# Loading q once, splitting streamed weights on chip, and larger k, v and w_out transfers in a linear-attention and feed-forward kernel

## The chip, the core and the metric

The kernel runs on one core of a Trainium2 chip. A core has TensorE (PE, matrix products), VectorE (DVE), ScalarE (ACT), GpSimd (POOL) and SyncE (SP); each works through its own instructions in order and waits for others by semaphores. Transfers between HBM and on-chip memory are issued by SyncE and GpSimd here and run on 16 shared transfer engines. The metric is device microseconds of one execution, the median of three runs.

## The reference

What is computed, cut to what matters (8 batches, 8 heads, 576 positions, head size 64; w_in is 512 x 2048 and w_out 2048 x 512, both float64 and read as pairs of 32-bit words):

```python
kv = np.einsum('bhsd,bhse->bhde', k, v)
out = np.einsum('bhsd,bhde->bhse', q, kv)
rms = np.sqrt(np.mean(out * out, axis=-1, keepdims=True) + 1e-06)
x = (out / rms * g_norm).transpose(0, 2, 1, 3).reshape(4608, 512)
h = x @ w_in
g = h * np.tanh(np.log1p(np.exp(h)))      # mish
return g @ w_out
```

## The kernel before

**Two parts.** The first part makes x from q, k and v, multiplies it by w_in, applies mish and stores g to HBM (gd, gp). The second part reads g back and multiplies it by w_out. The tokens lie in 9 tiles of 512; tile 0 is done whole, tiles 1 and 2 singly, and tiles 3 to 8 in three pairs. The second part works on 18 groups of 256 tokens.

**Seven products.** Both matmuls use a scheme with seven block products instead of eight (A11, S1, S2, S4, A12, S3, A22 of the left side against T1, T3, T2, T4, B11, B21, B22 of the right side). T1, T2, T3 and T4 are differences of the weight's four blocks. Each factor is kept as a high and a low half: `split` casts the high half on ScalarE and subtracts it on VectorE (L210 to L212), and a product has three terms of them.

**Places.** The first part is a row of 256 places, one block product in each. Place 0 is the first product of w_in; tile 0 takes places 0 to 31, tiles 1 and 2 take 28 each, and each pair 56 (from 88, 144 and 200). All other work (a load, a transpose, a cast) is a named step, and the table `WHEN` gives each step its place; what stands at negative places comes ahead of the first product. The table alone sets the order of the instructions on every engine; nothing is reordered later. Names: `k3.mul0` is the product of k and v of batch 3 for the first four heads, `x4.1.transpose` a step of tile 4 for the second four heads, `w5.load` a block of w_in, `o3.load` a chunk of w_out, `s1.4` a streamed w_in.

**The weights.** w_in has 8 blocks of columns. Four forms of each (B11, B21, T4, B22) stay on chip in `wfb`. The three others (T1, T3 and T2) stay for six blocks in pages `wfa` and `wfc`; blocks 6 and 7 share theirs with the stream. Each block's split forms, 12 x 128 columns, are stored to HBM (`wid`) by GpSimd (L283, L284). For each pair of tiles six blocks are streamed back: `stream` (L288) issues two transfers straight into the pages of blocks 6 and 7, high and low halves as they are, once TensorE is done with the page. w_out is read in 16 chunks of 128 x 512 (L231), scaled by ScalarE (L222), joined from word pairs by VectorE (L217 to L219), differenced (L225 to L227), and stored to HBM (`wod`) by three GpSimd transfers each (L316 to L318).

**Attention.** k and v come in pieces of 128 x 576 (L327), with three buffers each. q of a tile comes from tile 2 on as `qs`: VectorE's transpose (L446) works on 32 x 32 squares, so each 32 partitions hold one half of the head's 64 columns, and q is loaded twice, shifted by 32 columns (L429, eight transfers where a tile spans two batches). The 1/rms row `fl` (ScalarE, ln and exp, L509 and L510) is stored to `rd` (L514), read back spread over the partitions (L520), and multiplied into x by VectorE (L528).

**Queues.** SyncE issues the loads, the stores of 1/rms and the loads of what they spread; GpSimd issues the stores of g (L723, L728, L731; L669 for tile 0), of `wid` and of `wod`. The tiles for mish, `ula`, `ulb` and `ur`, have two buffers each. `put_in` (L725) adds into them on VectorE, ScalarE applies mish (L208).

Of the kernel before, what the change touches and what calls it, by code (L numbers as in the profile page):

```python
# [8 lines left out]
F32 = mybir.dt.float32  # L9
F32R = mybir.dt.float32r  # L10
U32 = mybir.dt.uint32
# [6 lines left out]
T1, T3, T2, T4, B11, B21, B22 = range(7)  # L18
# [6 lines left out]
    "w1.load": -57.761, "w1.scale": -57.665, "kv.a": -56.646, "rows.a": -56.517, "w0.load": -55.073, "kv.mul.a": -54.701,  # L25
    "rows.b": -50.685, "constants": -49.286, "kv.b": -48.206, "kv.keep.a": -46.532, "x0.0.transpose": -44.158,
# [95 lines left out]
def linear_attention_rms_mish_ffn(  # L122
# [169 lines left out]
    def weight_out(c, h):  # L292
# [14 lines left out]
        def join():  # L307
            join_words(st["x"], st["w"])
# [999 lines left out]
```

## Time and profile before

| What | Value |
|---|---|
| Runs | 819.5, 820.7 and 824.51 us, median 820.7 |
| Profiled execution | 819.2 us, its span 817.4 us |
| Busy share of the span | TensorE 96%, VectorE 71%, ScalarE 54%, GpSimd 13% |
| Granted TensorE clock, mean | 0.988 |
| Moved | 181.09 MB |

The profiled execution is one execution on the chip, its span from the first to the last instruction. Matmuls are pipelined, so a busy TensorE is not TensorE at its peak. A line number is that of the kernel before. "Idle before" is the time in which an engine had nothing to do just ahead of an instruction, and the name behind the arrow is what ended it. The granted clock is a share of full speed, 2.4 GHz; 0.5 of it is 1.2 GHz.

### The profile page before, as it was taken

The numbers are of one execution on the slowest core, as the hardware profiler recorded it, in microseconds if no ns is written. First come the engines' busy times: TensorE is split into PE (matmuls) and PEld (weight loads), VectorE is DVE, ScalarE is ACT, GpSimd is POOL, SyncE is SP. The second block draws the span as 40 slices with busy tenths as digits, with TensorE's granted clock in tenths as the row PEclk, the third lists the DMA queues.
The fourth block names the chain that finished last, engine by engine and source line by source line (L and its number), as shares of the span: only waits on it lengthen the run. The fifth ranks groups of instructions, "written<-read, shape, count | busy, mean of one in ns | idle before, by whom it ended". The sixth has DMA issues, their size and how long they took to land.

```text
span 817.4 us, 14052 instructions
## 1 busy us (share of the span) xinstructions
PE 781.9 (96%) x5456; PEld 660.7 (81%) x5456; DVE 578.5 (71%) x714; ACT 441.6 (54%) x641; POOL 104.0 (13%) x191
## 2 busy tenths in 40 slices
PE   3999999989998999899999999999999999999997
PEld 2677898879766777678888998888888888888886
DVE  2887846468436785658436788888888888877885
ACT  3877765746635475466547664444444444445442
POOL 1021321122213222332111100000000000000000
PEclk9999999989999999999999999999999999999999
DMA  9998979999998968989679653344444444444401
GB/s 269 278 326 268 360 273 317 286 272 304 321 317 275 318 223 285 291 314 321 231 255 340 209 194 129 129 141 128 146 130 152 134 126 154 134 140 152 142 27 52
DMA packets 118434, 181.09 MB, mean 222 GB/s; under 512 B 18720, under 2 KB 80160, under 8 KB 118368
## 3 DMA queue, kind: packets, MB, share of 16 engines
q1 hardware_dynamic: 102848, 128.74, 51.4%
q0 software_dynamic: 15424, 51.39, 16.8%
q8 instruction: 43, 0.70, 0.4%
q14 instruction: 23, 0.19, 0.1%
q10 hardware_dynamic: 96, 0.07, 0.0%
HBM read 119.21 MB, written 60.95 MB: 220 GB/s over the span
## 4 chain that ended last, share of the span: by engine, by line
PE 80%; DMA 9%; issue 5%; ACT 2%; SPq 1%; DVE 1%; POOL 1%; ACTq 0%; POOLq 0%; DVEq 0%
PE a L1061 15%; PE bc L1061 11%; PE a L690 10%; PE a L1066 8%; PE bc L690 7%; PE bc L1066 6%; PE a L680 5%; PE bc L680 3%; PE a L658 3%; PE q L1209 2%; PE bc L658 2%; PE x L468 2%; DMA wod<-wx 2%; DMA qs<-in_q_dram 2%; DMA wfa<-wid 2%
## 5 line engine op out<-in xcount | busy, mean ns | idle before, releaser
L725 DVE TENSOR_TENSOR ula<-bc,ula 128x512 f32<-128x512 f32 x32 | 22.0, 687 | 43.5 <-PE bc L690 24.8
L208 ACT ACTIVATE ur<-ur 128x1024 f32<-128x1024 f32 x32 | 33.9, 1059 | 31.2 <-DVE ur L725 31.1
L690 PE MATMUL bc<-wfa,wfa 128*128 128x512 f32 x144 | 37.4, 395 | 6.3 <-DVE ula L725 3.6
L690 PE MATMUL a<-wfc,wfc 128*128 128x512 f32 x96 | 34.9, 405 | 3.7 <-ACT ula L607 3.4
L690 PEld LDWEIGHTS bc<-wfa,wfa 128*128 128x128 f32 x144 | 26.8, 188 | 13.8 <-DVE ula L725 4.1
L690 PE MATMUL a<-wfa,wfb 128*128 128x512 f32 x144 | 37.1, 393 | 0.0
L690 PE MATMUL bc<-wfc,wfb 128*128 128x512 f32 x144 | 36.9, 392 | 0.0
L620 ACT COPY ur<-a 128x512 f32<-128x512 f32 x32 | 18.8, 586 | 32.8 <-PE a L690 28.3
L211 ACT CAST wfa<-g 128x1024 fp32r<-128x1024 f32 (+1 forms) x24 | 23.8, 998 | 21.5 <-PE a L1066 7.8
L211 ACT CAST wfc<-wfb 128x1024 fp32r<-128x1024 f32 x23 | 24.0, 1051 | 20.9 <-PE a L1066 11.7
L212 DVE TENSOR_TENSOR wfa<-g,wfa 128x1024 fp32r<-128x1024 f32 (+1 forms) x24 | 27.5, 1154 | 9.4 <-ACT wfa L211 9.4
L208 ACT ACTIVATE ula<-ula 128x512 f32<-128x512 f32 x32 | 20.2, 633 | 25.3 <-DVE ula L725 25.0
L690 PE MATMUL a<-pc,wfb 128*128 128x512 f32 x96 | 33.9, 393 | 0.0
L690 PE MATMUL a<-pb,wfa 128*128 128x512 f32 x96 | 33.7, 391 | 0.0
L690 PE MATMUL bc<-pa,wfb 128*128 128x512 f32 x96 | 33.6, 390 | 0.0
L690 PEld LDWEIGHTS a<-wfa,wfb 128*128 128x128 f32 x144 | 26.7, 188 | 8.2 <-issue 2.5
L690 PEld LDWEIGHTS bc<-wfc,wfb 128*128 128x128 f32 x144 | 27.1, 189 | 6.8 <-issue 1.1
L211 ACT CAST wfa<-wfb 128x1024 fp32r<-128x1024 f32 x19 | 19.9, 1052 | 21.5 <-PE a L1066 15.5
L725 DVE TENSOR_TENSOR ur<-a,ur 128x512 f32<-128x512 f32 x32 | 21.9, 685 | 11.8 <-PE a L690 8.1
L1116 DVE TENSOR_TENSOR ur<-ow 128x1024 f32<-128x1024 f32 x16 | 19.6, 1225 | 14.1 <-ACT ow L1113 14.1
L212 DVE TENSOR_TENSOR wfa<-wfb,wfa 128x1024 fp32r<-128x1024 f32 x19 | 23.1, 1220 | 8.9 <-ACT wfa L211 8.9
L211 ACT CAST wfc<-g 128x1024 fp32r<-128x1024 f32 x17 | 17.7, 1051 | 17.2 <-PE a L1066 11.7
(524 smaller groups left out, 2454.7 us busy)
## 6 DMA issues: line engine op xcount, KB each, us to landing
gp<-ur POOLq DMA_DIRECT2D x24, 512.0 KB, 6.2
g<-gp SPq DMA_DIRECT2D x12, 1024.0 KB
wfb<-gp SPq DMA_DIRECT2D x12, 1024.0 KB
wfa<-wid SPq DMA_DIRECT2D x18, 512.0 KB
w<-in_moe_w_out_dram SPq DMA_DIRECT2D x32, 256.0 KB
km<-in_k_dram SPq DMA_DIRECT2D x28, 288.0 KB
vm<-in_v_dram SPq DMA_DIRECT2D x28, 288.0 KB
gp<-ula POOLq DMA_DIRECT2D x24, 256.0 KB, 4.7
```

What stands on the lines that cost most here:

```text
L208: nc.scalar.activation(o, i, AF.Mish)
L211: nc.scalar.copy(hi, src)
L212: nc.vector.tensor_sub(lo, src, hi.bitcast(F32))
L468: nc.tensor.matmul(st["x"][a][half(o), c], kv[r], st["q"][r, a, c], start=True, stop=True)
L620: then(t + 4, lambda: nc.scalar.copy(dst(st, "12"), st["a"]))
L658: nc.tensor.matmul(banks[m], w[:, a, kc, :], xf[b][:, kc], start=r == kc == s == 0, stop=(r == kc == 1 and s == 2), skip_group_check=True,)
L680: nc.tensor.matmul(bank[:, jj * TH:(jj + 1) * TH], w[:, a, kc, :], xf[b][:, kc], start=first and jj == kc == s == 0, stop=(kc == 1 and s = ...
L690: nc.tensor.matmul(bank, w[:, a, kc, :], xf[b][:, kc], start=first and kc == s == 0, stop=(kc == 1 and s == 2), skip_group_check=True,)
L725: nc.vector.tensor_add(o, bank_view(st, block, bank), o)
L1061: nc.tensor.matmul(bank.rearrange("p (s h n) -> p s h n", s=2, h=2), gf[0][:, c], wo_form(c, right), start=first and c == 0, stop=False, s ...
L1066: nc.tensor.matmul(halves(bank)[:, 0], gf[1][:, c], wo_form(c, right)[:, 0], start=False, stop=c == NF2 - 1, skip_group_check=True)
L1116: nc.vector.tensor_add(st["o"].rearrange("p r (c n) -> p (r c) n", c=2), a[:, :, 0], a[:, :, 1])
```

## The change

**q.** Each 32 partitions' first half loads the whole run of 64 columns; a new step `double` (GpSimd, two copies of 32 x 32 x 32) writes the second half from it. Transfers per load fall from eight to four, or from four to two where a tile lies in one batch.

**Streamed w_in.** `wid` keeps the three differences whole (6 x 128 columns, stored from `wd`), and `split_ring` makes both halves on chip, into one ring page `tr` of blocks 6 and 7. For the first two pairs a step `load` brings them into a page `ws` of its own; for the third into the lower half of the ring page itself.

**k, v and w_out.** k and v are 128 x 2 x 576 in one transfer, two buffers for k and one for v. w_out comes in 8 chunks of twice the size, each scaled and joined in two steps, with one buffer, and is stored by two transfers; the forms lie as 7 x 256 columns, so a form's order on the right side changes (B21 ahead of B11).

**1/rms.** It is stored four times over and read as rows of both heads' 1024 values.

**Places.** Every entry of `WHEN` is new, among them the step that loads ScalarE's table for ln and exp. The core of the diff:

```diff
-    "table.exp": -43.37, "x0.0.turned": -42.175, "w1.join": -41.998, "w2.load": -38.422, "w4.load": -38.247,
+    "table.exp": 139.787, "s1.1.load": 140.314, "f5.1.0": 140.744, "x7.0.project": 140.822, "f5.4.0": 141.698,
...
-    kvp = part1.enter_context(tc.tile_pool(name="kvp", bufs=3))
+    kvp = {name: part1.enter_context(tc.tile_pool(name=name + "p", bufs=n)) for name, n in (("k", 2), ("v", 1))}
...
+    def split_ring(n, src):
+        t = ring(n).rearrange("p (s n) -> p s n", s=2)
+        split(t[:, 0], t[:, 1], src)
...
         def store():
-            c = j % 2 * FORM
-            nc.gpsimd.dma_start(wid[j][:, 0:PAGE], page(f"wfa{j}").bitcast(F32))
-            nc.gpsimd.dma_start(wid[j][:, PAGE:], page(f"wfc{j // 2}")[:, c:c + FORM].bitcast(F32))
+            nc.gpsimd.dma_start(wid[j], st["d"][:, 0:3].rearrange("p f n -> p (f n)"))
...
-    def stream(j, n):
-        nc.sync.dma_start(page(f"wfa{NF2 - 2 + n}").bitcast(F32), wid[j][:, 0:PAGE])
-        nc.sync.dma_start(page(f"wfc{NQ - 1}")[:, n * FORM:(n + 1) * FORM].bitcast(F32), wid[j][:, PAGE:])
+    def stream(j, n, staged):
+        st = {}
         def load():
+            st["t"] = pools["ws"].tile([P, 6 * P], F32, name="ws") if staged else ring(n)[:, 6 * P:].bitcast(F32)
+            nc.sync.dma_start(st["t"], wid[j])
+
+        return load, lambda: split_ring(n, st["t"])
...
+    def kv_load(name, b, n):
+        t = kvp[name].tile([P, 2, 9 * D], F32, name=name + "m")
+        src = (k if name == "k" else v)[b, 4 * n:4 * n + 1]
+        nc.sync.dma_start(t, bass.AP(src.tensor, src.offset, [[9 * D, P], [2 * S * D, 2], [1, 9 * D]]))
+        return t
...
-            for i in (0, 2, 1, 3):
+            for i in (0, 2):
...
-                    src = q[b, 4 * u + i // 2, s0:s0 + 1, R * (i % 2):]
-                    src = bass.AP(src.tensor, src.offset, [[run, R], [(3 - 2 * (i // 2)) * S * D, 2], [1, run - R]])
+                    src = q[b, 4 * u + i // 2, s0:s0 + 1]
+                    src = bass.AP(src.tensor, src.offset, [[run, R], [(3 - i) * S * D, 2], [1, run]])
...
+        def double():
+            t = qs[u].rearrange("p a (c d) -> p (a c) d", d=D)
+            for i in (0, 2):
+                nc.gpsimd.tensor_copy(t[(i + 1) * R:(i + 2) * R, :, 0:R], t[i * R:(i + 1) * R, :, R:])
...
-    step("pools.wx", start(3), pools_of(("w64", 2), ("wx", 1)))
+    step("pools.wx", start(3), pools_of(("w64", 1), ("wx", 1), ("ws", 1)))
```

New places that the prediction speaks of: the products k2.mul1 34.88, k3.mul0 39.55 and k3.mul1 44.25; k5.mul1 81.43, k6.mul0 85.13 and k6.mul1 90.17. The splits s0.6 at 135.93, s1.4 at 178.72, s1.5 at 185.47 and s2.2 at 220.70, whose forms are first used at places 138, 180, 187 and 222. The loads of q and their copies x6.0 at 91.09 and 91.65, x7.0 at 114.03 and 114.98, x8.1 at 159.65 and 161.66.

**How it moves instructions.** First SyncE's queue around the 1/rms of tiles 3 and 4 (rd is the row's store, fh and fa its spread; rd_111 is tile 3's row before, rd_114 after). Before:

```order
L429 DMA qs<-in_q_dram 32x2x608
L429 DMA qs<-in_q_dram 32x2x352
L514 DMA rd_112<-fl 2x512 x4
L520 DMA fh<-rd_111 64x2x512 x2
L520 DMA fa<-rd_112 64x2x512 x2
L231 DMA w_2128<-in_moe_w_out_dram 128x2x256 x2
```

After:

```order
L558 DMA rd_114<-fl 8x1x512 x4
L565 DMA fh<-rd_114 64x1x1024 x2
L467 DMA qs<-in_q_dram 32x2x640
L467 DMA qs<-in_q_dram 32x2x384
L467 DMA qs<-in_q_dram 32x2x640
L467 DMA qs<-in_q_dram 32x2x384
L325 DMA w_2005<-in_moe_w_out_dram 128x1024 x2
L565 DMA fa<-rd_114 64x1x1024 x2
```

The spread of tile 3's first half stood behind a q load of eight and another tile's stores; it now stands behind its own stores, and a q load of four behind it.

Second, ScalarE ahead of the first product (fa and fh hold squares and then 1/rms of tile 0's two halves; the first product needs pa, and wfb_308 before, wfb_332 after). Before:

```order
L474 ACTIVATE fa<-x_229 128x1024
L211 CAST wfb_247<-wfa_133 128x4x256
L504 ACTIVATE fa<-a,eps 128x512 x2
L505 ACTIVATE fa<-fa 128x1024
L211 CAST wfb_308<-wfa_227 128x4x256
L369 COPY kv_120<-s_119 128x128
L452 COPY wfa_142<-ss 128x512
L452 COPY wfa_142<-bc 128x512
L211 CAST pa_327<-x_305 128x1024
```

After:

```order
L547 ACT_TABLE_LOAD
L547 ACTIVATE fa<-a,eps 128x512 x2
L548 ACT_TABLE_LOAD
L548 ACTIVATE fa<-fa 128x1024
L407 COPY kv_123<-s_122 128x128
L214 CAST wfb_296<-wfa_216 128x4x256
L495 COPY wfa_151<-ss 128x512
L495 COPY wfa_151<-bc 128x512
L225 ACTIVATE wfa_304<-w_228 128x1024
L214 CAST pa_318<-x_293 128x1024
L520 ACTIVATE fh<-bc 128x512 x2
L225 ACTIVATE wfa_328<-wfb_231 128x1024
```

Two table loads have come in, and the scaling of the weight for the first product, which stood ahead of the squares, now stands behind both copies of q.

Third, GpSimd's queue at the end of tile 2 and in the first pair. Before:

```order
L731 DMA gp_89<-ur 128x1024
L723 DMA gp_89<-ulb 128x512
L316 DMA wod_101<-wx 128x128
L317 DMA wod_101<-wx 128x2x128
L318 DMA wod_101<-w_2479 128x512
L728 DMA gp_89<-ula 128x512
```

After:

```order
L776 DMA gd_91<-ur 128x1024
L472 COPY qs<-qs 32x32x32 x2
L768 DMA gd_91<-ulb 128x2x256
L773 DMA gp_92<-ula 128x512
L776 DMA gp_92<-ur 128x1024
L355 DMA wod_104<-w_2485 128x1024
L356 DMA wod_104<-wx 128x768
L768 DMA gp_92<-ulb 128x512
```

Where three stores of converted w_out stood between two stores of g, there are two now, and at other places a pair of copies of q.

## Rows read from the trace of the kernel before

**Rows 1.** The page, part 1: busy us, share of the span, instructions
```profile
PE 781.9 (96%) x5456; PEld 660.7 (81%) x5456; DVE 578.5 (71%) x714; ACT 441.6 (54%) x641; POOL 104.0 (13%) x191
```

**Rows 2.** Table by stage: length, busy us by engine, PEclk, transfers' share, GB/s
```profile
0.00:31.50 31.50, 17.23 (x187) 11.63 (x188) 13.24 (x15) 16.37 (x21) 2.62 (x15) 1.00 0.97 294
31.50:345.00 313.50, 296.58 (x2689) 242.12 (x2688) 206.76 (x293) 188.47 (x294) 73.55 (x126) 0.97 0.92 293
345.00:460.00 115.00, 114.85 (x512) 93.95 (x511) 68.47 (x104) 71.10 (x113) 26.71 (x48) 1.00 0.80 278
460.00:817.40 357.40, 353.27 (x2073) 312.95 (x2071) 290.06 (x305) 165.71 (x215) 1.08 (x2) 1.00 0.43 134
```

**Rows 3.** TensorE's waits: waited for, us in total, times, longest
```profile
PE s L351 <- DMA wfb<-in_v_dram: 11.1, 1, 11.1
PE bc L680 <- ACT ur L612: 3.9, 1, 3.9
PE bc L690 <- DVE ula L725: 3.6, 1, 3.6
PE a L690 <- ACT ula L607: 3.4, 1, 3.4
PE bc L690 <- DMA wfa<-wid: 2.7, 2, 1.9
PE ss L362 <- DMA vm<-in_v_dram: 2.5, 1, 2.5
```

**Rows 4.** The same table, just behind four of these waits
```profile
124.60:130.00 5.40, 5.40 (x99) 4.43 (x100) 2.58 (x3) 0.08 (x1) 0.00 (x0) 0.68 1.06 279
178.00:186.00 8.00, 7.95 (x45) 7.95 (x46) 7.58 (x10) 3.38 (x7) 2.25 (x4) 0.63 0.97 290
247.60:254.00 6.40, 6.36 (x99) 4.59 (x100) 5.45 (x8) 3.32 (x5) 2.69 (x5) 0.73 1.06 308
334.60:340.00 5.40, 5.33 (x18) 4.32 (x19) 2.48 (x5) 2.65 (x6) 2.88 (x5) 0.73 0.83 240
```

**Rows 5.** SyncE's queue, then the chain of waits, 157 to 178: start, us, what
```profile
159.87 6.52 SPq L429 DMA_DIRECT2D qs<-in_q_dram  x8
...
170.82 4.29 DMA fh<-rd
```

**Rows 6.** The chain of waits, 205 to 250
```profile
235.90 5.55 issue
241.46 5.43 DMA gp<-ulb
```

**Rows 7.** The chain of waits, 100 to 180
```profile
118.69 5.75 DMA vm<-in_v_dram
```

**Rows 8.** The page, part 6: transfers, how many, KB each
```profile
wfa<-wid SPq DMA_DIRECT2D x18, 512.0 KB
```

**Rows 9.** Groups of ScalarE and VectorE (busy us, mean ns); ScalarE in order of time
```profile
L211 ACT CAST wfb<-wfb 128x768 fp32r<-128x768 f32 x1 | 0.8, 845 | 0.0
L212 DVE TENSOR_TENSOR wfb<-wfb 128x768 fp32r<-128x768 f32 x1 | 1.0, 951 | 0.0
L217 DVE TENSOR_SCALAR wfa<-wfa 128x1024 uint32<-128x1024 uint32 x8 | 5.5, 691 | 17.7 <-ACT wfa L222 17.7
...
161.16 1.28 ACT L508 ACT_TABLE_LOAD   x1
162.60 0.69 ACT L509 ACTIVATE fl<-ss,eps 128x512 f32<-128x512 f32 x1 [0.15 <-issue]
```

**Rows 10.** Groups of GpSimd: busy us, mean ns, idle before
```profile
masks.py:199 POOL TENSOR_SCALAR_AFFINE_SELECT ident<-ident 128x128 f32<-128x128 f32 x1 | 0.3, 287 | 0.1
L791 POOL MEMSET ones<- 128x128 f32 x1 | 0.2, 194 | 0.0
```

**Rows 11.** ScalarE and TensorE in order of time, first 40 us
```profile
23.92 1.06 ACT L505 ACTIVATE fa<-fa 128x1024 f32<-128x1024 f32 x1
...
30.48 3.33 PE L658 MATMUL a<-pa,wfb 128*128 128x512 f32 x12
```

More of the change, by code (lines that the diff above doesn't have):

```diff
@@ L17 @@
 A11, S1, S2, S4, A12, S3, A22 = range(7)
-T1, T3, T2, T4, B11, B21, B22 = range(7)
+T1, T3, T2, T4, B21, B11, B22 = range(7)
 PROD = ((A11, B11, "a"), (S1, T1, "c"), (A22, T4, "p"), (S2, T2, "a"), (A12, B21, "b"), (S4, B22, "c"), (S3, T3, "a"))
@@ L24 @@
 WHEN = {
-    "w1.load": -57.761, "w1.scale": -57.665, "kv.a": -56.646, "rows.a": -56.517, "w0.load": -55.073, "kv.mul.a": -54.701,
-    "rows.b": -50.685, "constants": -49.286, "kv.b": -48.206, "kv.keep.a": -46.532, "x0.0.transpose": -44.158,
[90 rows of a table removed]
+    "kv.a": -58.068, "constants": -56.889, "rows.a": -56.704, "w1.load": -56.033, "kv.mul.a": -55.141, "kv.b": -54.793,
[93 rows of a table added]
 }
@@ L235, in forms, with ring, in_ring @@
         return t.rearrange("p (f s m n) -> p f s m n", s=2, m=2, n=P)
+    rings = {}
+    def ring(n, dtype=F32R, fresh=False):
+        if fresh or n not in rings:
+            rings[n] = wfp.tile([P, 3 * FORM], dtype, name=f"tr{n}")
+        return rings[n]
+    def in_ring(t):
+        return t.rearrange("p (s f m n) -> p s f m n", s=2, f=3, n=P)
+    def split_ring(n, src):
+        t = ring(n).rearrange("p (s n) -> p s n", s=2)
+        split(t[:, 0], t[:, 1], src)
     def w_form(j, f, streamed=None):
@@ L239, in w_form @@
             return forms(wb[j])[:, RESIDENT.index(f)]
-        j = j if streamed is None else NF2 - 2 + streamed
+        n = j - (NF2 - 2) if streamed is None else streamed
+        if n >= 0:
+            return in_ring(ring(n))[:, :, f]
         return forms(page(f"wfc{j // 2}"))[:, j % 2] if f == T2 else forms(page(f"wfa{j}"))[:, int(f == T3)]
@@ L255, in scale @@
         def scale():
-            st["x"] = page(f"wfa{j}", F32, True)
+            st["x"] = ring(j - (NF2 - 2), F32, True)[:, 0:PAGE] if j >= NF2 - 2 else page(f"wfa{j}", F32, True)
             scale_words(st["x"], st["w"])
@@ L275, in sums @@
         def sums():
-            page(f"wfa{j}", F32R, True)
-            parts(forms(page(f"wfa{j}")), st["d"][:, 0:2])
-            parts(forms(page(f"wfc{j // 2}"))[:, j % 2:j % 2 + 1], st["d"][:, 2:3])
+            if j >= NF2 - 2:
+                ring(j - (NF2 - 2), F32R, True)
+                split_ring(j - (NF2 - 2), st["d"][:, 0:3].rearrange("p f n -> p (f n)"))
+            else:
+                page(f"wfa{j}", F32R, True)
+                parts(forms(page(f"wfa{j}")), st["d"][:, 0:2])
+                parts(forms(page(f"wfc{j // 2}"))[:, j % 2:j % 2 + 1], st["d"][:, 2:3])
@@ L292, in weight_out, with load @@
-    def weight_out(c, h):
+    def stream(j, n, staged):
         st = {}
-        whole = wod[c][:, h]
         def load():
-            srcs = []
+            st["t"] = pools["ws"].tile([P, 6 * P], F32, name="ws") if staged else ring(n)[:, 6 * P:].bitcast(F32)
+            nc.sync.dma_start(st["t"], wid[j])
+        return load, lambda: split_ring(n, st["t"])
+    def weight_out(c):
+        st = {}
+        def load():
+            st["w"] = pools["w64"].tile([P, 2, 8 * P], U32, name="w64")
@@ L315, in store @@
-        def store():
-            nc.gpsimd.dma_start(whole[:, B11:B11 + 1], st["x"][:, 0:1])
-            nc.gpsimd.dma_start(whole[:, B21:B22 + 1], st["x"][:, 1:4:2])
-            nc.gpsimd.dma_start(whole[:, T1:T4 + 1], st["d"])
-        return load, scale, join, differences, store
-    def kv_load(b, hp):
-        ts = []
-        for name, src in (("km", k), ("vm", v)):
-            t = kvp.tile([P, 9 * D], F32, name=name)
-            src = src[b, 2 * hp:2 * hp + 1]
-            nc.sync.dma_start(t, bass.AP(src.tensor, src.offset, [[9 * D, P], [1, 9 * D]]))
-            ts.append(t)
-        return ts
+                nc.sync.dma_start(st["w"][:, 1 - fh], w_out[f0:f0 + P, :])
@@ new lines, in words, with blocks, scale, join @@
+        def words(r):
+            return st["w"].rearrange("p f (r n t) -> p r f n t", r=2, t=2)[:, r]
+        def blocks(r):
+            return st["x"][:, r]
+        def scale(r):
+            if "x" not in st:
+                st["x"] = pools["wx"].tile([P, 2, 2, G], F32, name="wx")
+            nc.scalar.mul(blocks(r), words(r)[:, :, :, 1].bitcast(F32), 2.0 ** -112)
+        def join(r):
+            w, t = words(r), blocks(r).bitcast(U32)
+            low, high = w[:, :, :, 0], w[:, :, :, 1]
+            nc.vector.tensor_single_scalar(t, t, 3, ALU.logical_shift_left)
+            nc.vector.scalar_tensor_tensor(t, high, 0x80000000, t, ALU.bitwise_and, ALU.bitwise_or)
+            nc.vector.scalar_tensor_tensor(t, low, 29, t, ALU.logical_shift_right, ALU.bitwise_or)
@@ L331, in half @@
+        return {
+            "load": load, "scale0": lambda: scale(0), "scale1": lambda: scale(1), "join0": lambda: join(0),
+            "join1": lambda: join(1), "diff": differences, "store": store,
+        }
+    def kv_load(name, b, n):
[3 more added lines that the diff above has]
+        return t
     def half(o, turned=False):
@@ L528, in normalize @@
                 nc.vector.tensor_mul(o, o, st["rr"])
-        return {f.__name__: f for f in (load, transpose, turned, project, square, scaled, sums, rstd, keep, spread, normalize)}
+        return {f.__name__: f for f in (load, double, transpose, turned, project, square, scaled, sums, rstd, keep, spread, normalize)}
     def x_block(j, r, h):
@@ L853, in linear_attention_rms_mish_ffn @@
             step(f"k{b}.keep{n}", t + made[n] + 1, lambda b=b, n=n: k_keep(b, n))
-        for p in range(4):
-            step(f"k{b}.load{p}", t + loads[p], lambda b=b, p=p: k_load(b, p))
+            for m, name in enumerate("kv"):
+                step(f"k{b}.{name}{n}", t + loads[n] + 0.001 * m, lambda name=name, b=b, n=n: k_load(name, b, n))
     def attention(j, t, steps):
@@ L862, in attention @@
             else:
+                if j >= T32 and "transpose" in names:
+                    step(f"x{j}.{u}.double", t + n - 0.01, lambda u=u: do(j, u, "double"))
                 for m, name in enumerate(names):
@@ L923, in linear_attention_rms_mish_ffn @@
     step("pools.xt", t1 + 18, pools_of(("xt", 1)))
-    step("pools.wx", start(3), pools_of(("w64", 2), ("wx", 1)))
-    places = [start(3) + n for n in (13, 20, 26)] + [start(j) + n for j in (4, 5, 6) for n in (3, 8, 13, 20, 26)][:13]
-    for i, t in enumerate(places):
-        def chunk(i=i, s=0):
-            if s == 0:
-                conv["out", i] = weight_out(i // 2, i % 2)
-            conv["out", i][s]()
-        for s, n in zip(range(5), (-5, 0, 0.01, 1, 2)):
-            step(f"o{i}.{('load', 'scale', 'join', 'diff', 'store')[s]}", t + n, lambda i=i, s=s, chunk=chunk: chunk(i, s))
+    step("pools.wx", start(3), pools_of(("w64", 1), ("wx", 1), ("ws", 1)))
+    for c in range(NF2):
+        t = start(3) - 11 + 15 * c
+        conv["out", c] = weight_out(c)
+        for n, name in zip((0, 5, 5.1, 6, 6.1, 7, 8), ("load", "scale0", "join0", "scale1", "join1", "diff", "store")):
+            step(f"o{c}.{name}", t + n, lambda c=c, name=name: conv["out", c][name]())
     gs = [{"s": s, "f": {}, "mm": None} for s in range(NG)]
@@ L965, in place2 @@
                 wb[int(name[3:])] if name.startswith("wfb")
-                else up.tile([P, FORM], F32R, name="ula") if name == "ula" else page(name)
+                else up.tile([P, FORM], F32R, name="ula") if name == "ula" else ring(int(name[2:])) if name.startswith("tr") else page(name)
             )
@@ L1156, in linear_attention_rms_mish_ffn @@
         for n in range(1, NF2 - 1):
-            step(f"s{i}.{n}", start(SINGLE + 2 * i) + 7 * n, lambda j=order[n + 1], n=n: stream(j, (n + 1) % 2))
+            t = start(SINGLE + 2 * i) + 7 * n
+            for (name, m), f in zip((("load", -6 if i < 2 else -0.5), ("split", -0.4 if i < 2 else 1)), stream(order[n + 1], (n + 1) % 2, i < 2)):
+                step(f"s{i}.{n}.{name}", t + m, f)
     for t in sorted(t for t in plan if t < 0):
```

74 lines of the change are left out of this document (37 added, 37 removed), and 183 rows, old and new, of tables (WHEN, homes).

## The prediction

> **What bounds the kernel now.** I read the busy shares first, then a table by stage, then the list of what TensorE waited for, then the chain of waits around its longest stops. TensorE is busy 781.9 us of a span of 817.4 [rows 1]. By stage [rows 2]: in the first 31.5 us TensorE works 17.2; from there to 345 it loses 16.9 us, with the transfer engines at 0.92 of their time; from 345 to 460, where they have fallen to 0.80, it loses 0.15. Behind 460 us (the second matmul, which keeps its instructions) it loses 4.1, with the transfer engines at 0.43. So the kernel is bound by TensorE, and what a change of transfers and places can give is the start and the stops up to 345 us.
>
> TensorE's own list names the stops [rows 3]: 11.1 us for the first k and v, and in the middle 3.9, 3.6, 3.4, 2.7 (twice a wait, 1.9 the longest) and 2.5: **16.1 us**. After four of them the granted clock is low [rows 4]: 0.68, 0.63, 0.73 and 0.73 over 5.4, 8.0, 6.4 and 5.4 us, that is stretches at 1.2 instead of 2.4 GHz behind a stop, worth 1.7 + 3.0 + 1.7 + 1.5 = **7.9 us**. Together the middle holds 24.0 us that a perfectly fed kernel would not spend. The start is a separate sum.
>
> Why it stops. The 3.9 us at 174 to 178: the queue of SyncE issues eight pieces of a q load for 6.52 us, and only behind them the piece of 1/rms that a normalize waits for, which needs 4.29 us more; VectorE is held in its order by that normalize [rows 5]. The 3.6 us at 244 to 248: GpSimd's queue stands 5.55 us at a store of converted w_out, the store of a mish tile behind it lands 5.43 us after its issue, and VectorE needs that tile's room [rows 6]. The chain of the 3.4 us at 331 to 335 reads the same way, through the room of a chunk of w_out. The 2.7 us are two streamed w_in pages that came late, the 2.5 us a v load that came 5.75 us after its issue [rows 7].
>
> **The change part by part.** The sum is made against the profiled execution: 819.2 us, of which the span is 817.4. The median of the three runs, 820.7, is 1.5 above that, and I add it at the end.
>
> *Fewer bytes.* A streamed w_in is 12 x 128 columns of 4 bytes, 786 KB, moved eighteen times, the first 512 KB of it by the transfers of [rows 8]; whole instead of in two parts it is half: 7.1 MB less read, and 3.1 MB less stored for the eight w_in blocks. q is read once instead of nearly twice: some 6 MB less, and four issues per load instead of eight in full segments. That is 16 MB of the some 133 that the rates of [rows 2] give for the first 460 us, an eighth, and would bring 0.92 near the 0.80 at which TensorE no longer waited. w_out comes in 8 chunks instead of 16, with two stores each instead of three, so GpSimd's queue has 16 places of the kind of [rows 6] instead of 48. In the new order the first half of 1/rms of tile 3 stands directly behind its store, ahead of the q load that was in front of it. Each of the five causes is thus weakened or gone: I book **-24.0**, and what comes back as new terms (bounds: 0, if the waits are of order and not of bytes, and -24.0).
>
> *Splitting on chip.* Eighteen splits, each a cast of 845 ns on ScalarE and a subtraction of 951 ns on VectorE [rows 9]: 15.2 and 17.1 us of work. Between 31.5 and 460 us ScalarE works 259.6 of 428.5 us and VectorE 275.2 [rows 2], so they fit beside TensorE. The cover is gone where a split is recorded little ahead of its product. Two thirds of them (the first two pairs of tiles) load into a page of their own some products early, which takes the late pages of [rows 3] away; but the splits s0.6, s1.4, s1.5 and s2.2 stand 1.3 to 2.1 places ahead of their first use. 256 places lie between 30.48 us [rows 11] and 460, 1.68 us each, so they have 2.2 to 3.5 us for 1.8 us of work that stands behind other work on both engines. I take one of them late by all of it, **+2** (bounds 0 and four times 1.8, 7.2).
>
> *v with one buffer.* k and v come as 128 x 2 x 576 in one transfer; k has two buffers, v one. So v of a pair of heads can't be asked for until the product before it has read its v. At four of them (k3.mul0, k3.mul1, k6.mul0, k6.mul1) the next product stands 3.7 to 5 places behind, 6.2 to 8.4 us, and the nearest row has 5.75 us from issue to landing for half these bytes [rows 7]. I take one stop of the size of the old one with its clock, 2.5 + 1.7: **+4.2** (bounds 0 and four, 16.8).
>
> *GpSimd copies.* 28 copies of 32 x 1024 elements, two ahead of each VectorE transpose. The trace has no such copy. Nearest are 287 ns and 194 ns for 128 columns [rows 10]: eight times the larger is 2.3 us, and if all of the smaller were fixed cost a copy is 0.2. Between them 1.2, so 34 us on an engine that is busy 104 of 817. What counts is order: a copy waits for its q, and a mish store behind it waits too. I take two thirds of one stop like that of [rows 6], 3.6 + 1.7: **+3.5** (bounds 0 and three such stops, 15.9).
>
> *The start.* k and v now go ahead of w_in's 1.05 MB, which at the 294 GB/s of [rows 2] is 3.6 us earlier than 11.1. But the step that loaded one table for both ln and exp has moved from place -43 to 139.8, and each 1/rms of tile 0 now loads a table twice, 1.28 us each [rows 9]: exp, which ended at 24.98 [rows 11], ends at 24.98 - 3.6 + 2.6 = 24.0. Behind it ScalarE has, in the new order, a copy of 128 columns, a cast of 1024, two copies of 512 and only then the scaling, 1024, of the w that the first product needs; at the 1.1 us per 1024 columns of [rows 9] that is 3.4, 27.4. VectorE joins it with one pass of 0.69 and two of 1.27 (30.6), and a last cast and subtraction take 1.1 and 1.27: 33.0, against 30.48 now [rows 11]. **+2.5** (bounds -0.1, if the loads hide in waits, and +5.1, if the second pair lies on the path too).
>
> The Trainium skill (ScalarE: Activation LUTs, What ACT_TABLE_LOAD costs) gives 1283 ns for the load and 1380 ns of drain with it. The trace agrees on the first; of the drain it shows little, since the ln at 162.60 starts 0.16 us behind a load that ends at 162.44 [rows 9]. By the page's total the start would be 2.8 us longer and the sum below 2.8 higher.
>
> The forms of w_out as two runs of 256 columns, the four copies of 1/rms in HBM (0.4 MB) and the larger k transfers I book at nothing: the matmuls of the second part keep their number and columns, and the rest lies in the transfers' spare time.
>
> Sum: -24.0 + 2.0 + 4.2 + 3.5 + 2.5 = **-11.8**, so 807.4 for such an execution and with 1.5 some **809** for the median.
>
> **The rivals.**
> *Late v.* If three of the four narrow places stop, +8.4 to the sum: 817. For it: the margins above, and a queue that also holds q. Against: the queue is shorter by q's four issues. Chance 0.15.
>
> *Copies hold VectorE.* If VectorE can't read its second operand while GpSimd's copy reads, 28 x 1.2 = 34 us are taken from VectorE; it idles a third of the time, so if a quarter of it is on the path, +8: 817. That is what the Trainium skill (SBUF — State Buffer, Who interferes with whom) says of VectorE instructions with two SBUF inputs; no row here has a reading GpSimd instruction beside one. Chance 0.08.
>
> *The change doesn't do what it says.* If the stops come from the order of queues and not from their load, the new places have as many: -24.0 falls to about -11 and the time is 822. For it: [rows 6] is a wait for VectorE, not for bytes. Chance 0.05.
>
> *GpSimd's queue becomes the bound (slower).* Each of 14 pairs of copies stands between mish stores and waits for its q. For x6.0, x7.0 and x8.1 it is recorded 0.6 to 2 places behind the load, and eight issues of the old q load alone took 6.52 us [rows 5]. A stop there costs 3.6 + 1.7 = 5.3. To pass 829 us it needs four beyond my sum; with five of the 14 the time is 835. Against: at most places a store has several places' time until its room is needed. Chance 0.12.
>
> **How the numbers follow.** My forecast (most stops gone, one or two new) has 0.60 and spans 800 to 812.5. About 1% is what a measurement here can tell from no change, 8.2 us. Late v, VectorE held and unmoved stops lie within it: same 0.28. Slower 0.12. The range leaves out the slower case and the last twentieth of gain (all bounds at their best, 797): **799 to 827**.
>
> **What would show it.** Right: the transfer share of 88 to 345 near 0.82; TensorE's waits in the middle under 8 us in sum, with two low-clock stretches or fewer; no wait on a stream's transfer between 178 and 345; the first product near 33 us with five table loads by the second exp; GpSimd's copies 1 to 1.5 us. Wrong: waits on v's transfer at three places; mish stores standing behind a copy while ScalarE or VectorE wait for their rooms; TensorE waits on casts of the ring; a share of 0.90 that stays.

## The result, and the profile after

The changed kernel takes **794.57 us** (median of 4 runs, 794.01 to 796.45) against 820.1 for the kernel before beside it: a ratio of 0.969, interval 0.964 to 0.973. The forecast was 809 with a range of 799 to 827: the direction was right, the time lies below the range, and the gain of 25.5 us is more than twice the 11.7 that the forecast took off the 820.7 of before. The profiled execution takes 794.12 us, its span is 792.3, which is 25.1 less than the 817.4 of before.

Where the 25 us went is read from three places in the two traces: the first product of w_in starts at 28.31 instead of 30.48 us, the pairs of tiles begin at 187.53 instead of 197.22, the second part's loop of groups begins at 455.54 instead of 480.71, and from there to the end both kernels need the same 337 us. So 2.2 us come from the start, 7.5 from tiles 0 to 2 and 15.5 from the pairs.

The page of after, part 1, as in [rows 1] (busy us, share of the span, instructions):

```profile
PE 772.8 (98%) x5456; PEld 654.8 (83%) x5456; DVE 601.9 (76%) x713; ACT 461.4 (58%) x661; POOL 112.3 (14%) x179
```

The table by stage of after, columns as in [rows 2]; its third stage ends at 435 instead of 460 because everything lies some 25 us sooner there:

```profile
0.00:31.50 31.50, 18.84 (x194) 12.04 (x195) 13.08 (x14) 20.02 (x24) 2.62 (x15) 1.00 0.92 277
31.50:345.00 313.50, 310.89 (x2793) 255.26 (x2792) 241.58 (x315) 215.06 (x328) 91.83 (x131) 1.00 0.84 279
345.00:435.00 90.00, 90.00 (x403) 74.68 (x402) 57.45 (x84) 60.74 (x98) 16.78 (x31) 1.00 0.65 230
435.00:792.30 357.30, 353.10 (x2071) 312.77 (x2070) 289.77 (x303) 165.59 (x214) 1.08 (x2) 1.00 0.42 134
```

In the second row TensorE now works 310.9 of 313.5 us (296.6 before), its granted clock is 1.00 (0.97), and the transfer engines' share fell from 0.92 to 0.84. VectorE and ScalarE work more (241.6 for 206.8, 215.1 for 188.5), in part because the stage now reaches further into the kernel, and behind 31.5 us TensorE waits 0.5 us in all for them. The last row is nearly that of before.

TensorE's waits in after, as in [rows 3]:

```profile
PE s L389 <- DMA wfb<-in_v_dram: 6.4, 1, 6.4
PE bc L511 <- ACT wfa L495: 1.5, 1, 1.5
PE a L534 <- ACT fa L517: 1.2, 1, 1.2
PE x L511 <- ACT fh L497: 1.1, 1, 1.1
PE x L484 <- DMA qs<-in_q_dram: 1.1, 1, 1.1
PE ss L534 <- ACT fh L520: 1.0, 1, 1.0
PE a L703 <- ACT wfb L214: 0.9, 1, 0.9
PE s L400 <- DMA vm<-in_v_dram: 0.8, 1, 0.8
```

All but two of these lie in the start. The two, 1.1 us for a q load at 45 us and 0.8 for a v at 183, are what is left of the middle's 16.1, and behind neither does the clock fall: it is granted in full until the last product is done. That is one execution; of the other three the slowest, 796.45 us, has a mean clock of 0.996, which would be some 6 us at 1.2 GHz at a place that isn't recorded.

### The profile page after: what moved, and what is told of

Its sections match the earlier page's. It is cut to its first block, busy times and chain, and to the rows that moved or that the text cites. A ratio compares the mean times of both kernels' runs of the same rounds, so it can differ in the third digit from the quotient of the medians.

```text
span 792.3 us, 13807 instructions
## 1 busy us (share of the span) xinstructions
PE 772.8 (98%) x5456; PEld 654.8 (83%) x5456; DVE 601.9 (76%) x713; ACT 461.4 (58%) x661; POOL 112.3 (14%) x179
## 4 chain that ended last, share of the span: by engine, by line
PE 92%; DMA 2%; DVE 2%; SPq 1%; ACT 1%; issue 1%; DVEq 0%
PE a L735 16%; PE a L1106 16%; PE bc L1106 12%; PE bc L735 12%; PE a L1111 8%; PE bc L1111 6%; PE a L725 6%; PE bc L725 4%; PE q L1256 3%; PE x L511 2%; PE bc L703 2%; PE a L703 2%; PE s L400 2%; SPq L434 1%; PE ss L541 1%; DMA vm<-in_v_dram 1%
## 5 line engine op out<-in xcount | busy, mean ns | idle before, releaser
L211 ACT ACTIVATE ur<-ur 128x1024 f32<-128x1024 f32 x32 | 33.9, 1059 | 25.3 <-DVE ur L770 25.1
L472 POOL COPY qs<-qs 32x1024 f32<-32x1024 f32 x28 | 33.0, 1180 | 43.4 <-DMA qs<-in_q_dram 39.6
L735 PE MATMUL bc<-wfa,tr 128*128 128x512 f32 x144 | 36.7, 390 | 0.0
L735 PE MATMUL a<-wfc,tr 128*128 128x512 f32 x96 | 33.8, 393 | 0.0
L735 PE MATMUL a<-pb,tr 128*128 128x512 f32 x96 | 33.7, 392 | 0.0
L214 ACT CAST wfa<-wfb 128x1024 fp32r<-128x1024 f32 x19 | 19.9, 1052 | 21.5 <-PE a L1111 15.5
L735 PEld LDWEIGHTS bc<-wfa,tr 128*128 128x128 f32 x144 | 26.9, 188 | 6.4 <-issue 0.8
L770 DVE TENSOR_TENSOR ur<-bc,ur 128x512 f32<-128x512 f32 x32 | 21.9, 684 | 9.7 <-ACT ula L211 4.2
```

The source lines that it names most:

```text
L211: nc.scalar.activation(o, i, AF.Mish)
L214: nc.scalar.copy(hi, src)
L472: nc.gpsimd.tensor_copy(t[(i + 1) * R:(i + 2) * R, :, 0:R], t[i * R:(i + 1) * R, :, R:])
L735: nc.tensor.matmul(bank, w[:, a, kc, :], xf[b][:, kc], start=first and kc == s == 0, stop=(kc == 1 and s == 2), skip_group_check=True,)
L770: nc.vector.tensor_add(o, bank_view(st, block, bank), o)
```

## The experiments

All times are medians; each is compared with 794.6 of the changed kernel. The kernel before, measured beside the runs, took 817.2 to 820.5 us, so a difference of 2 or 3 us between two runs says little. First the question whether fewer bytes or new places took the stops away, from both sides.

**e1, e2, e3: the old bytes at the new places.** In e1 q's load has its four issues for the second halves again and GpSimd's `double` is empty:

```diff
-            for i in (0, 2):
+            for i in (0, 2, 1, 3):
...
-                nc.gpsimd.tensor_copy(t[(i + 1) * R:(i + 2) * R, :, 0:R], t[i * R:(i + 1) * R, :, R:])
```

> The changed kernel with q's second halves loaded from HBM again (four more issues for each of the 14 loads, some 6 MB) and no GpSimd copies; all places as in the changed kernel. Theory A (the stops in the middle went because the transfer queues carry less): a part of them comes back, one stop of about 4 us with its low clock, 5 to 6 us, so about 800 us, and the transfer share of 178 to 345 us rises from 0.83 to about 0.86. Theory B (the new places alone removed the stops): within 2 us of 794.6. Theory C (the GpSimd copies hold VectorE on the path): faster than 794.6 by 1 to 4 us.

In e2 w_in's streamed forms are stored as high and low parts and loaded straight into the ring, so the page `ws` that let two thirds of them come early is given up as well:

```diff
-            nc.sync.dma_start(st["t"], wid[j])
+            nc.sync.dma_start(ring(n)[:, 0:PAGE].bitcast(F32), wid[j][:, 0:PAGE])
+            nc.sync.dma_start(ring(n)[:, PAGE:].bitcast(F32), wid[j][:, PAGE:])
```

> The changed kernel with w_in's streamed forms stored and streamed as high and low parts again (10 MB more, eight more stores and 18 more transfers, loaded straight into the ring at the places that the streams had before); no splits on chip while streaming; everything else at the places of the changed kernel. Theory A (fewer bytes removed the stops): late pages come back, 2.7 us with 1.7 of low clock and about one stop more, so 799 to 804 us. Theory B (the other places alone): within 2 us of 794.6. If the 18 splits cost anything on the path of the changed kernel, it is faster than 794.6.

e3 is both.

> Both of the former: q loaded twice and the streams whole in high and low parts, all other places as in the changed kernel. Theory A (bytes): most of the 22 us that the middle lost comes back, 806 to 818 us, transfer share of 178 to 345 us near 0.90, stops in the middle over 8 us in sum. Theory B (places): at most 4 us above 794.6, with stops in the middle under 5 us in sum.

Measured: e1 798.5 (797.4 to 802.0), e2 803.0 (802.1 to 803.6), e3 **817.0** (814.3 to 819.2; ratio to before 0.997, interval 0.995 to 0.999). q's 6.5 MB cost 4.0 us, the streams' 10.2 MB 8.4, both 22.4, more than the sum: the kernel has slack for one of them, not for both. Theory A holds against B, with "bytes" standing for more than bytes: q's load has twice the issues, and the streams have lost their page. TensorE's waits in e3, three largest (the third is the start):

```profile
PE bc L770 <- DMA tr<-wid: 9.3, 3, 4.9
PE s L437 <- DMA vm<-in_v_dram: 8.0, 2, 5.5
PE s L426 <- DMA wfb<-in_v_dram: 6.4, 1, 6.4
```

The stops are back, but at other places than in before: late streams, and v. Ahead of the 5.5 us SyncE's queue reads (start, us, what):

```profile
118.90 8.65 SPq L504 DMA_DIRECT2D qs<-in_q_dram  x8
127.65 0.71 SPq L403 DMA_DIRECT2D vm<-in_v_dram  x1
```

A q load of eight issues occupies the queue for 8.65 us, and v stands behind it. In after the same two loads read:

```profile
119.38 2.75 SPq L467 DMA_DIRECT2D qs<-in_q_dram  x4
122.23 0.39 SPq L366 DMA_DIRECT2D vm<-in_v_dram  x1
```

**e5, e6: bytes alone, issues alone.** e3 has more issues as well as more bytes. e5 adds transfers that nobody reads, one behind each q load and each streamed page, from HBM to HBM, and a second store behind that of each w_in block:

```diff
+            nc.sync.dma_start(tc.dram_tile([P, 992], F32, name=f"xq{j}{u}"), again)
...
+            nc.sync.dma_start(tc.dram_tile([P, 6 * P], F32, name=f"xs{j}{n}{staged}"), wid[j])
```

> The changed kernel with bytes alone added, in few transfers: behind each q load one more transfer of 508 KB from q to a scratch in HBM, behind each streamed page one more of 393 KB, behind each store of a w_in block a second store of the same size; nothing reads the scratch, all places stay. About 16 MB, as much as e3_both added, but 14 + 18 issues on SyncE and 8 on GpSimd. Theory A (bytes make transfers late): a large part of the 22 us of e3_both comes back, 804 to 818 us, with waits on v and stream transfers. Theory D (what stops is SyncE's queue, by the number of its issues): under 799 us.

e6 splits transfers in two:

```diff
-                    nc.sync.dma_start(t[i * R:(i + 1) * R, :, c0:c0 + run], src)
+                    for a in range(2):
+                        half_ = bass.AP(src.tensor, src.offset + a * (3 - i) * S * D, [[run, R], [1, run]])
+                        nc.sync.dma_start(t[i * R:(i + 1) * R, a, c0:c0 + run], half_)
```

> The changed kernel with issues alone added: each q load in eight issues instead of four, each streamed page in two instead of one, of half the size, in the same bytes and packets; all places stay. Theory A (bytes): within 2 us of 794.6. Theory D (the number of issues): each q load again takes 4 us or more on SyncE's queue instead of 2.0 to 2.5, waits on v come back, 799 to 812 us.

Measured: e5 **808.7** (806.8 to 812.6), e6 799.0 (795.4 to 800.0). In e5 a q load still takes some 2 us of SyncE's queue, but the v behind it needs 9.82 us to land by the chain of waits:

```profile
123.76 1.73 SPq L469 DMA_DIRECT2D qs<-in_q_dram  x4
...
126.19 9.82 DMA vm<-in_v_dram
```

The v that after waits for lands in 7.42:

```profile
175.80 7.42 DMA vm<-in_v_dram
```

In e6 the bytes are those of after and the eight issues of a q load take 3.6 to 6.9 us of the queue:

```profile
176.38 6.85 SPq L469 DMA_DIRECT2D qs<-in_q_dram  x8
```

So issues lengthen the queue. That bytes lengthen the landing is likely and not shown: the two v's waited for in e5 took 9.82 and 9.28 us, but with the bytes of after such a v took from 6.94 (e6) to 8.65 (e11), in e7 9.8 passed from such an issue at 192.82 to the product that waits, and in e3 a v took 6.29 and another 9.13.

The bytes bring 14.1 us back, with waits of 6.0 us on v at two places (the extra stores of w_in blocks also hold VectorE's room for 7.9 us in all, and so v is asked for at 126.19 instead of 122.23). The issues bring 4.4: the profiled execution of e6, the fastest, has no stop over 0.6 us behind the first group, so what the other three lost isn't shown. Together that is 18.5 of e3's 22.4. By the ratios to the kernel before beside each (0.989, 0.976 and 0.997, for 0.969 of after) they are 17, 6 and 23 us, so no part need be left over.

Why issues and landings act on each other stands in before's chain of waits ahead of the stop at 174:

```profile
162.03 7.17 DMA qs<-in_q_dram
...
169.22 0.22 SPq L514
```

The store of 1/rms (L514) waits until a piece of q has landed that it has nothing to do with. In the traces SyncE's transfers report their landing on eight semaphores in turn, and an issue waits until the earlier transfer on its semaphore has landed. A load of eight pieces thus needs eight earlier landings, whatever they carry. In e6 two pieces of the load above wait for a v and a k:

```profile
SPq L469 <- DMA vm<-in_v_dram: 1.5, 1, 1.5
SPq L469 <- DMA km<-in_k_dram: 0.6, 1, 0.6
```

In before the q loads at L429 wait 29 us in all for other tensors' landings, in after those at L467 not once. That fits q and the streams costing more together than their sum; no run changes the number of semaphores alone, so it is argued.

**e16: the kernel before, in its own order, with fewer bytes, and four issues less in each q load but the first.**

```diff
-            for i in (0, 2, 1, 3):
+            for i in (0, 2, 1, 3) if j == T32 and u == 0 else (0, 2):
...
-        nc.sync.dma_start(page(f"wfa{NF2 - 2 + n}").bitcast(F32), wid[j][:, 0:PAGE])
+        nc.sync.dma_start(page(f"wfa{NF2 - 2 + n}")[:, 0:FORM].bitcast(F32), wid[j][:, 0:FORM])
```

> The kernel before, in its own order, with bytes taken away (left out: q's second halves after the first load, and half of each streamed w_in page and of each stored w_in block, so that those halves keep what was there): some 6 + 7 + 3 MB less, as in the change, with 48 q issues less; no copy, no split, no new place. Theory A (the load on the transfers makes the stops, whatever the order): most of the 24 us goes, 796 to 805 us. Rival (the stops of GpSimd's queue and of w_out's rooms are of order): 806 to 814 us, with the stops at 244 and 331 us left.

Measured: **799.1** (798.5 to 801.6), 164.4 MB moved in place of 181.1 (the changed kernel moves 164.8). All stops of [rows 3] behind the start are gone or small, those too that I had read as stops of order, the store in GpSimd's queue and the room of a w_out chunk:

```profile
PE s L351 <- DMA wfb<-in_v_dram: 10.7, 1, 10.7
PE bc L682 <- ACT ur L614: 1.6, 1, 1.6
```

So lighter and fewer transfers alone, in the old order, are worth some 20 of the 25 us. A q load behind 100 us, four issues now, takes 1.8 to 2.7 us of SyncE's queue here (once 4.0).

**e12, e15: the new transfers in the old order.** All of the changed kernel's code, with the 305 steps behind place 60 at their former places; in e15 w_out's chunks at the new ones.

```diff
+WHEN.update({"k5.mul0": 77.073, "x6.0.load": 97.157, ..., "f7.6.1": 207.755})
```

> The changed kernel with the 305 steps that lie behind place 60 in both tables at their former places (k and v of a pair of heads at that of its first load, a chunk of w_out at those of the two half chunks that it replaces, a copy one place ahead of its transpose; streams keep their new places, which have no counterpart): the new transfers in the old order. Theory A (the bytes alone took the stops away): 794 to 800 us. Theory B (the new places were needed as well): 803 us or more, with stops of over 8 us in sum behind 100 us, though the transfer share of 178 to 345 us stays near 0.83.

> e12_oldplaces with the steps of w_out's chunks back at the places of the changed kernel (only the first chunk's load, 73.3, and its conversion, 77.0 to 78.0, lie up to three places later): all other steps behind place 60 in the old order. In e12_oldplaces the chain of waits at its long stops runs from a chunk's store through the load into the one room to ScalarE's scaling. Theory (only w_out's chunks, with one room for twice the size, needed new places; the bytes did the rest): 794 to 800 us. Rival (the old order stops the new transfers elsewhere too, at GpSimd's copies or v): 804 us or more, with waits for ScalarE's or VectorE's outputs left over.

Measured: e12 **853.7** (849.4 to 855.7), e15 **827.6** (825.7 to 827.9): slower than the kernel before, by 4.1 and 1.1%. The table of the stage from 31.5 to 345 us, in this order, e16, e1, e5, e3, e15, e12 (columns as above: TensorE's busy time stands first, the transfers' share last but one):

```profile
31.50:345.00 313.50, 308.89 (x2777) 252.02 (x2776) 217.60 (x315) 200.26 (x311) 82.93 (x141) 1.00 0.84 268
```
```profile
31.50:345.00 313.50, 307.85 (x2779) 252.72 (x2778) 227.90 (x310) 213.44 (x324) 59.09 (x103) 1.00 0.90 296
```
```profile
31.50:345.00 313.50, 300.30 (x2715) 245.08 (x2714) 227.33 (x299) 206.24 (x313) 92.98 (x131) 0.98 0.90 308
```
```profile
31.50:345.00 313.50, 293.75 (x2687) 238.77 (x2687) 204.05 (x280) 196.53 (x298) 58.17 (x101) 0.98 0.90 298
```
```profile
31.50:345.00 313.50, 292.53 (x2671) 238.66 (x2669) 218.08 (x286) 195.50 (x302) 87.73 (x121) 0.98 0.79 256
```
```profile
31.50:345.00 313.50, 283.13 (x2607) 229.37 (x2605) 207.15 (x268) 188.79 (x289) 83.53 (x113) 0.96 0.75 243
```

Two ways to lose are told apart here. In e5 and e3 TensorE stops while the transfers are at 0.90. In e15 and e12 it stops though they are at 0.79 and 0.75: these are waits of order. The share alone tells neither: e1 is at 0.90 too and loses little, for what counts is whether a transfer that TensorE needs comes late. e12's longest stops hang on w_out's one room; the chain of waits ahead of its last, 7.3 us long, is a store, the next load into the room and a scaling on ScalarE that stands right behind it:

```profile
380.98 2.99 DMA wod<-w
...
384.41 6.78 DMA w<-in_moe_w_out_dram
...
391.30 0.66 ACT wx L643
391.96 0.48 ACT ur L972
392.44 0.04 issue
392.48 5.49 PE a L1042 x12
```

e15's longest, 5.2 us at 240, is a split. ScalarE stands at the cast of a staged page whose transfer SyncE could only issue behind a q load that held its queue for 4.75 us, and a copy that TensorE needs stands behind it (ScalarE in order of time, with its idle time in brackets):

```profile
237.55 0.83 ACT L471 CAST tr<-ws 128x768 fp32r<-128x768 f32 x1 [7.01 <-DMA ws<-wid]
238.28 1.05 ACT L468 ACTIVATE ur<-ur 128x1024 f32<-128x1024 f32 x1
239.24 0.57 ACT L909 COPY ula<-a 128x512 f32<-128x512 f32 x1
```

Theory B of e12 and the rival of e15 hold: the new code needs new places, and not for w_out alone.

**e7, e10: GpSimd's copies.** Three times over, and 26 of 28 left out:

```diff
-            for i in (0, 2):
+            for i in (0, 2) * 3:
```
```diff
-            for i in (0, 2):
+            for i in (0, 2) if j == T32 and u == 0 else ():
```

> The changed kernel with each of the 28 GpSimd copies made three times over: 56 copies of 1.18 us more, 66 us of GpSimd's time. Theory (the copies lie beside idle time of GpSimd and VectorE): within 2 us of 794.6. Rival (copies hold VectorE's instructions with two SBUF inputs, and stores behind them): if VectorE loses 0.8 us for each copy that it meets, and a quarter of that is on the path, 56 x 0.8 / 4 = 11 us, 806.

> The changed kernel without 26 of its 28 GpSimd copies (left out: the second halves of q then stay those of the first load, so that part of the attention isn't computed from its own q); q is still loaded once, all places as in the changed kernel. If the copies as they are cost nothing on the path: within 1 us of 794.6. If they cost in proportion to what the threefold copies cost (32 us for 56 more), 26 of them are worth 15 us: 780. Between: the chain from q through a copy to VectorE's transpose has little room, 1 to 4 us faster.

Measured: e10 793.2 (792.4 to 796.3), e7 **826.8** (825.4 to 828.7). As they stand the copies cost 1.4 us by the medians, with overlapping spreads; 56 more cost 32, three times what my rival had. The price isn't proportional: the slack ends between one and three times. In e7 TensorE waits for transposes and tile scalings of VectorE, and for outputs that stand behind a wait of VectorE, for a w_in store in GpSimd's queue (5.1 us) or for its own slower instructions:

```profile
PE x L511 <- DVE x L527: 4.5, 2, 2.9
PE x L511 <- DVE fl L489: 4.4, 3, 2.2
PE a L725 <- ACT ur L665: 4.2, 1, 4.2
PE bc L735 <- DVE ula L770: 2.5, 1, 2.5
```

with six stretches of low clock behind such stops. VectorE itself waits 10.5 us for the copies ahead of four transposes, which it never does in after. How much GpSimd's queue and how much the slower VectorE costs isn't separated.

**e4, e9, e11, e14: the start, and v.** e4 moves one step back:

```diff
+WHEN.update({"table.exp": -43.37})
```

> The changed kernel with one step moved: the table for ln and exp is loaded at its former place, -43.37, ahead of the first 1/rms, instead of at 139.8. In the profile of the changed kernel one of the two loads of 1.28 us in tile 0's first 1/rms lies behind a matmul (ScalarE waits there anyway), the other lies on the chain to the first product. Theory: the first product 1.3 us sooner, and the total 1 to 1.3 us shorter, 793.3 to 793.6. Rival 1: both pairs were on the path, 2.6 us, 792. Rival 2: the first product waits for transfers anyway, within 0.3 us of 794.6.

Measured 793.8 (793.0 to 797.1): the first product comes 0.4 us sooner (27.88), the first group of products ends 0.9 sooner, and later stops in its profiled execution (v late by 1.9 at 185, with the clock low for 3.4 behind it, among them) give it back. By the median between my theory and rival 2; the spreads overlap, and e11, which keeps this order up to there, ends the first group another 0.9 sooner, so 0.9 is also what two executions of one order differ by.

e9 also moves w0.scale and w0.join ahead of w1.blocks, w2.scale and w2.join behind the second 1/rms, and k5.mul1 to 82.9.

> The changed kernel with six steps of the start and two behind it moved: the table for ln and exp at its former place (-43.37); w0.scale and w0.join directly behind x0.0.normalize, ahead of w1.blocks (in the changed kernel w0 is in place near 20.1 us and is scaled at 22.78, behind 2 us of other work on ScalarE); w2.scale and w2.join behind the second 1/rms; k5.mul1 and k5.keep1 one product later (82.9), so that the next v has more time than the 0.84 us that it was late. Theory: the first product near 25.9 us instead of 28.31, no wait on v near 184, 790 to 792 us. Rival: the later products of the first group then wait for tile 0's second half, and the gain stays under 1 us: 793.5 or more.

Measured 796.4 (794.4 to 798.6). Neither move did what it was meant to. ScalarE reaches the scaling of w0 early and waits 1.79 us for its transfer, with the turned q behind it, so the first product comes at 28.66, though the first group still ends at 84.88 (86.25 in after). And k5.mul1 is the product that sets v's one buffer free: a product later, the wait of 0.8 us became 3.6, with the clock low for 6.8 us behind it.

e11 keeps the table at -43.37 and moves the product that waits:

```diff
+WHEN.update({"table.exp": -43.37, "k6.mul0": 86.5})
```

> The changed kernel with two steps moved: the table for ln and exp at its former place, and k6.mul0, the product that waited 0.84 us for v in the changed kernel, at 86.5 instead of 85.133, one product later (the run before this had delayed the release of v's buffer, k5.mul1, by one product instead, and its wait grew to 3.58 us). Theory (v's one buffer sets that wait: it is asked for when the product before has read it, and takes some 7 us to land): no wait on v near 184, low clock nowhere in the middle, 792.5 to 793.5 us. Rival: the wait moves to the next product with v, 794 to 797.

Measured 792.65 (791.8 to 794.4; ratio to before 0.967, interval 0.964 to 0.970, which overlaps that of the changed kernel). The v wait is 0.6 us, the clock never falls behind a stop, but a k is now waited for, 1.2 us at 99, where after has no wait: the rival holds in part. It is the fastest of these kernels, by less than these runs can tell.

e14 takes w1's products first.

> e11_best with the start in another order: the first group takes the products of w1 ahead of those of w0 (w1 is ready some 6 us before w0, which lands near 21 us), and the second half of tile 0 goes ahead of w0's split on ScalarE and VectorE. Theory (the first product waits for w0's chain of scale, three VectorE passes and cast): the first product near 24 us instead of 28.3, the end of the first group 1 to 3 us sooner, 790 to 792. Rival: the first group then waits for w0 and for tile 0's second half by as much, within 1 us of e11_best.

Measured 796.1 (795.2 to 797.6). The first product comes at 23.63 us, yet the first group ends at 88.05 (84.49 in e11): TensorE then waits, among others, 1.4 us for w0's cast and 1.6 behind a mish on ScalarE. The rival holds, and worse.

## Why the prediction was too small

**-24.0 for the stops in the middle: right.** After has 1.9 us of stops and no low clock there, so 22.1 of 24.0 are gone; e16 shows that the lighter and fewer transfers do it. That the causes of [rows 5] and [rows 6] read as waits for an order is no contradiction: the q load that filled SyncE's queue for 6.5 us was long by its issues (e6), and in e16 the same store of a mish tile stops nobody. [rows 6] I had also misread. GpSimd's queue stands those 5.55 us not at converted w_out but at the store of the mish tile itself, which waits for ScalarE:

```profile
241.46 0.54 POOL L723 DMA_DIRECT2D gp<-ulb  x1 [5.56 <-ACT ulb L208]
```

So the count of 48 stores falling to 16 was no reason for this stop to go.

**+2.0 for a split late, +4.2 for v, +3.5 for copies: the steps that failed.** None came at its price: no wait on the ring, 0.8 us on v, 1.4 by the medians for the copies. The mechanisms are real, each was made to appear: v and its one buffer in e3 (8.0 us of waits), e5 (6.0) and e9 (3.6), a late split in e15 (5.2), the copies in e7. But I priced v and the copies with stops of the loaded kernel, 2.5 and 3.6 us, each with its 1.7 of low clock (two thirds of the second for the copies), in the same sum in which I took those stops away: the load was counted gone in one line and present in two others, one of them a stop that I had misread. The split's 1.8 us are its own work, and that size is right (0.83 and 0.95 us in after); what failed there is that one of four would come late by all of it. That the places were set for the new steps counts as well: at the old ones they do cost (e15, e12).

For v the margin is thin, and that after's profiled execution shows so little of it is in part luck: there a landing of 7.42 us leaves a wait of 0.8, while in e4, whose v's stand at the same places, one of 8.50 leaves 1.9 with 1.7 of low clock, together 3.6 of the 4.2 that I had.

**+2.5 for the start: wrong, -2.2.** k and v landed at 6.42, 4.7 us sooner and not 3.6. Two table loads were booked at 2.6; in after they are

```profile
14.61 1.02 ACT L517 ACTIVATE fa<-x 128x1024 f32<-128x1024 f32 x1 [0.61 <-PE x L511]
15.65 1.28 ACT L547 ACT_TABLE_LOAD   x1
16.95 1.51 ACT L547 ACTIVATE fa<-a,eps 128x512 f32<-128x512 f32 x2
18.48 1.28 ACT L548 ACT_TABLE_LOAD   x1
19.77 1.06 ACT L548 ACTIVATE fa<-fa 128x1024 f32<-128x1024 f32 x1
```

The first lies beside TensorE's sums, for which ScalarE would wait anyway. The ln starts 1.3 us behind the square's end, as it does in before, so the first load costs nothing. The second has nothing beside it: in e4, without it, the exp ends at 19.81 instead of 20.83. So k and v came 1.1 us sooner than booked, one load of 1.3 was hidden, and the work from k and v to the square was 0.7 shorter; the exp ended at 20.8 and not at 24.0. Behind the exp I had 9.0 us of work to the first product, and it was 7.5; of the 1.0 that e4 gains at the exp, 0.4 is left at the first product. Five table loads by the second exp were forecast, and there are five.

**The rivals.** Late v and copies that hold VectorE are both in the trace, and both all but hidden. A bound by GpSimd's queue needs three times the copies, if it is the queue (e7, 827). That the stops come from order and not from load is ruled out by e16; that the new places alone took them away, by e3 (817 with the old transfers).

**The sum.** 819.2 - 22.1 - 2.2 is 794.9; the profiled execution took 794.1.

## What to carry to other kernels

When a change takes load off a shared resource, price its new steps with durations from a stage where that resource is less loaded, or the load is counted twice. Here that is 345 to 460 us of before: a store of `ulb` landed in 3.5 us by the median there and in 5.7 from 200 to 345; for a v, loaded earlier, no such row exists. Stops that look like bad order can be load: test by taking transfers away in the old order (e16) and by putting them back in the new (e3, e5). Slack is not proportional: the two parts of the bytes cost 4 and 8 us back, together 22, and copies that cost next to nothing once cost 32 us three times over, so a step that is free now says little of its double.

## What the runs showed of the hardware

The time that a load takes of SyncE's queue grows with its issues, and not evenly: behind 100 us, four pieces of a q load took 2.0 to 2.8 us in after, eight of half the size in the same bytes 3.6 to 6.9 in e6. At 3.6 none of the eight waits for another transfer's landing; at 6.9 two do, 2.1 us together.

A GpSimd copy of 32 x 1024 elements takes 1.03 us alone and up to 1.93 beside VectorE (mean 1.18; my estimate was 1.2). VectorE's instructions with two operands in SBUF become longer beside it; in after, VectorE and then GpSimd, in order of time:

```profile
283.77 1.21 DVE L614 TENSOR_TENSOR pc<-wfa,pb 128x1024 fp32r<-128x1024 f32 x1
284.90 2.06 DVE L614 TENSOR_TENSOR pd<-wfa,pc 128x1024 fp32r<-128x1024 f32 x1
286.88 0.68 DVE L770 TENSOR_TENSOR ur<-bc,ur 128x512 f32<-128x512 f32 x1
```
```profile
284.58 3.28 POOL L472 COPY qs<-qs 32x1024 f32<-32x1024 f32 x2 [1.18 <-DMA qs<-in_q_dram]
```

The first subtraction had begun ahead of the copy and keeps its 1.21 us; the second falls beside it and takes 2.06; the sum with an operand from PSUM (`bc`) keeps 0.68 to 0.69. That is the exclusion which the Trainium skill (SBUF — State Buffer, Who interferes with whom) describes. The trace agrees, at 0.85 us for one such meeting; by e10 26 of the 28 copies cost the kernel 1.4 us at the medians.

The Trainium skill (ScalarE: Activation LUTs, What ACT_TABLE_LOAD costs) adds a drain to a table load. The rows of the first 1/rms above show nothing of it: the ln starts 0.02 us behind the end of its load, the exp 0.01.
